# Another opening for a Fourier-mixing and mixture kernel: unfolded stage A, moves within SBUF, four real products, GpSimd for the weights

## The chip, the cores and the metric

The kernel runs on one core of a Trainium2 chip. The metric is device microseconds for one execution. TensorE (PE in the profile, with its weight loads as PEld), VectorE (DVE), ScalarE (ACT) and GpSimd (POOL) each follow an instruction stream of their own. All transfers are issued from SyncE's queue (SP), in order, and run on the core's 16 DMA engines.

## The reference, cut to what matters

Eight sequences of 3008 tokens with 256 features go through a real Fourier transform along the sequence, a complex 256x256 matrix with bias, a soft threshold and the inverse transform. Each token then goes through a two-layer network with a squared ReLU.

```python
X = np.fft.rfft(x, axis=1)                  # x: (8, 3008, 256)
Yr = Xr @ w_r - Xi @ w_i + b_r
Yi = Xr @ w_i + Xi @ w_r + b_i
Yr = np.sign(Yr) * np.maximum(np.abs(Yr) - 0.01, 0)     # Yi likewise
y = np.fft.irfft(Yr + 1j * Yi, n=3008, axis=1)
h = np.maximum(y.reshape(24064, 256) @ w_in, 0)         # w_in: 256 x 2048
out = h * h @ w_out                                     # w_out: 2048 x 256
```

`x`, `w_r`, `w_i` and the biases are float32; `w_in` and `w_out` arrive as float64 and are narrowed on the chip.

## The kernel before, in words

The transform of length 3008 = 47 x 64 is done in stages, each a small matmul with a table. **Stage A** transforms over the 47 indices n1: for a real sequence, 24 frequencies r are enough. **Stage B** transforms over the 64 indices n2; a *pair* is two of the 24 frequencies, so there are 12 pairs (`NPAIR`) for a batch. Then comes the **mix**, the complex matrix as three real products (`MIX`, with the matrices w_r, -w_r-w_i, w_i-w_r in `wmf`, and the sum of the components from `sum_x`), the bias and the threshold (`add_e` and what follows it), a turn of real and imaginary halves into partitions (`zh`), **stage C** (the inverse over n2, table `tM`) and **stage D** (`inverse` or `plan_d`, the inverse over n1). Between A and B (`scr1`, tensors `s<-eva`, `bin<-s`) and between C and D (`scr2`, `s<-evc`, `din<-s`) the data go through DRAM, since rows become partitions.

Before stage A, real sequences are *folded*: the host places rows n1 and 47-n1 side by side (`xp`: 13 groups of up to 24 x 5 = 120 partitions), and `fold` makes their sum and difference on VectorE (L214, L215), so that each part is one matmul with 120 rows.

The network runs in **rounds**. The 104 groups of 5 n2-values form 52 chunks of 470 columns; each chunk takes 8 rounds (`NU`), so there are 416 and two more for the lag. In a round, `mm1` multiplies the chunk (`xt`) with two blocks of `w_in` into `ph` (L186 to L188, three products of high and low float32r parts), `squares` and `sums` prepare seven products (`g`), their high part `gh` (L793) and low part `gl` (L801) follow in the next round, and `mm2` (`po`) multiplies them with seven sums of `w_out` blocks (`wo`) two rounds after the first. Stages A, B, C, D of the batches 2 to 7 (B to D of batch 1) are placed into these rounds by a plan written out by hand: `at(r, place, do)` puts a step in round r at one of the places load, a1, p1, v1, p2, a2, v2, and the loop at the end runs them in that order. p1 lies behind `mm1`, p2 behind `mm2`, a1 behind `gh`, a2 behind the round's squares, v2 last on VectorE. The loop is under `tc.manual_schedule()`: each engine gets its instructions in program order.

`start()` is the **opening**: everything that must be there before round 0. It loads tables and weights, does stages A to C of batch 0, stage A of batch 1, the inverse of the first chunk, and turns `w_in` and `w_out` into high and low parts. It is written as generators that are interleaved (`stages_b` in the middle, `weights` every second step, `stage_a(1)` from the last pair on and behind it), but it stands outside of `manual_schedule`, so the scheduler of the framework settles each engine's order. Its matmuls are plain float32 (L409, L223, L440, L456). A weight piece (512 KB of float64) takes one DMA, one `Abs` on ScalarE (L318), four integer operations on VectorE (L319 to L324), and then either a split in two (`w_in`, L180 and L181) or two copies, four differences and a split (`w_out`, L362 to L367, L180, L181), with ScalarE for casts and VectorE for the rest. There are eight pieces of each.

A DMA tile named `t`, `ev` or `w` in the text is a rotating buffer: a new use waits until the last use of that buffer is over. In PSUM the opening has eight banks (`pst`), the rounds have two for the stages (`ps_f`).

Of the kernel before, what the change touches and what calls it, by code (L numbers as in the profile page):

```python
# [34 lines left out]
P = 128  # L35
S = 3008
# [43 lines left out]

def _cs(num, den):

    num = np.asarray(num) % den
    ang = 2.0 * np.pi * num / den
    c, s = np.cos(ang), np.sin(ang)
    c = np.where((4 * num) % (2 * den) == den, 0.0, c)
    s = np.where((2 * num) % den == 0, 0.0, s)
    return c, s


def tables():
# [39 lines left out]
    return dict(t_a=ta.astype(np.float32), t_b=tb.astype(np.float32), t_m=tm.astype(np.float32),  # L131
# [15 lines left out]
def fft_mix_moe(ctx: ExitStack, tc: tile.TileContext, xp, w_r, w_i, b_r, b_i,  # L147
                w_in, w_out, t_a, t_b, t_m, t_d, sgn, outT):
    nc = tc.nc
    B = xp.shape[0]  # L150
# [24 lines left out]
    wi_ = [ctile(f"wi{k}", [P, 2, DFF], F32R) for k in range(2)]  # L175
    wo_ = []

    def split(src, hi, lo):

        nc.scalar.copy(hi, src)  # L180
        nc.vector.tensor_sub(lo, src, hi.bitcast(F32))  # L181
# [16 lines left out]
    def load_x(b, i, t):  # L198
        nc.sync.dma_start(out=t, in_=xp[b].rearrange("g p d -> p g d")[:t.shape[0], i, :])
# [76 lines left out]
    def start():  # L276

        with ExitStack() as own:
            sb = own.enter_context(tc.tile_pool(name="sb0", bufs=2))
            pp = own.enter_context(tc.tile_pool(name="ps0", bufs=8, space=bass.MemoryType.PSUM))  # L280

            def tl(tag, shape=(P, 512), dt=F32, bufs=2, name=None):
                return sb.tile(list(shape), dt, tag=tag, name=name or tag, bufs=bufs)
# [3 lines left out]

            tA = tl("tA", (120, 4, 120), bufs=1)
            tM = tl("tM", (P, P), bufs=1)
            wmf = [tl(f"wmf{k}", (P, 3, D), bufs=1) for k in range(2)]  # L290

            def load_mix():
                nc.sync.dma_start(out=tB[:, :5], in_=t_b[:, :5])
                yield
                wr = tl("ld", bufs=4, name="wr").rearrange("p (k e) -> p k e", k=2)
                wi = tl("ld", bufs=4, name="wi").rearrange("p (k e) -> p k e", k=2)
# [4 lines left out]
                nc.sync.dma_start(out=sg, in_=sgn)  # L301
                nc.sync.dma_start(out=tM, in_=t_m)
                yield
                for k in range(2):
                    nc.scalar.copy(wmf[k][:, 0], wr[:, k])
                    nc.vector.scalar_tensor_tensor(wmf[k][:, 1], wr[:, k], -1.0, wi[:, k],
                                                   op0=ALU.mult, op1=ALU.subtract)
                    nc.vector.tensor_sub(wmf[k][:, 2], wi[:, k], wr[:, k])
                nc.sync.dma_start(out=tB[:, 5:], in_=t_b[:, 5:])
                nc.sync.dma_start(out=tD, in_=t_d)  # L310
                yield

            def narrow(t, h):
# [4 lines left out]
                nc.scalar.activation(h, hi.bitcast(F32), AF.Abs)  # L318
                nc.vector.tensor_scalar(h, h, F_MIN, F_MAX, op0=ALU.max, op1=ALU.min)  # L319
# [7 lines left out]
            def load_w(src, use):  # L327

                h = tl("w32")
                if src.dtype == F32:  # L330
                    nc.sync.dma_start(
                        out=h.rearrange("p (f n) -> p f n", f=2) if len(src.shape) == 3 else h, in_=src)
                    yield
                else:
                    t = tl("w64", (P, 512, 2), U32)
# [6 lines left out]
                    narrow(t, h)  # L342
                use(h)

            def load_win():
                for c in range(DFF // 512):
                    for k in range(2):
                        s = slice(512 * c, 512 * c + 512)

                        def use(h, k=k, s=s):  # L350
                            split(h, wi_[0][:, k, s], wi_[1][:, k, s])

                        yield load_w(w_in[k * P:(k + 1) * P, s], use)

            def load_wout():
                wo_.extend(ctile(f"wo{k}", [P, NU, NPR, P], F32R) for k in range(2))
                wv = w_out.rearrange("(f p) e -> p f e", p=P)
                for j in range(NU):
                    def use(h, j=j):
                        a = h.rearrange("p (f e m) -> p f e m", f=2, e=2)  # L360
                        w7 = tl("w7", (P, NPR, P), bufs=1)
                        nc.scalar.copy(w7[:, 0:3:2], a[:, :, 0])  # L362
                        nc.scalar.copy(w7[:, 1], a[:, 1, 1])
                        nc.vector.tensor_add(w7[:, 4], a[:, 0, 1], a[:, 1, 1])
                        nc.vector.tensor_sub(w7[:, 6], w7[:, 4], a[:, 0, 0])
                        nc.vector.tensor_sub(w7[:, 5], a[:, 0, 0], a[:, 0, 1])
                        nc.vector.tensor_sub(w7[:, 3], a[:, 1, 0], w7[:, 6])  # L367
                        split(w7, wo_[0][:, j], wo_[1][:, j])

                    yield load_w(wv[:, 2 * j:2 * j + 2, :], use)  # L370

            def rolling(pieces):

                last = None
                for p in pieces:
                    next(p)
                    if last is not None:
                        for _ in last:
                            pass
                        yield  # L380
                    last = p
                for _ in last:
                    pass
                yield

            def stage_a(b):
                scratch1(b)
                if b == 0:
                    st = [const.tile([P, 8, 512], F32, tag=f"wo{k}", name=f"x0{k}") for k in range(2)]
                    xv = xp[b].rearrange("g p d -> p g d")  # L390
                    for g0, g1 in ((0, 1), (1, 2), (2, 4), (4, 6), (6, 8), (8, 10), (10, 12), (12, 13)):
                        n = NR * GROUPS[g0][1]
                        k = g0 // 8
                        nc.sync.dma_start(out=st[k][:n, g0 - 8 * k:g1 - 8 * k, :], in_=xv[:n, g0:g1, :])
                    yield
                for i, (g, w) in enumerate(GROUPS):
                    n = NR * w
                    tab = 0 if w == W else 2
                    if b == 0:
                        t = st[i // 8][:n, i % 8, :]  # L400
                    else:
                        t = tl("ld", bufs=4, name="xin")[:n]
                        load_x(b, i, t)
                    f = tl("f")[:n]
                    fold(f, t)
                    o = pst("psa")[:n]
                    for c in range(2):
                        cs = slice(c * D, c * D + D)
                        nc.tensor.matmul(o[:, cs], tA[:n, tab + c, :n], f[:, cs], start=True, stop=True)  # L409
                    e = tl("ev", bufs=4, name="eva")[:n]  # L410
                    nc.scalar.copy(e, o)
                    store_a(b, i, e)
                    yield

            def stages_b():
                scratch2(0)
                xs, zs, got = {}, {}, {}

                def load(i):
                    got[i] = tl("ld", bufs=4, name="bin")  # L420
                    load_b(0, i, got[i])

                load(0)
                load(1)
                for i in range(NPAIR + 2):
                    if i + 2 < NPAIR:
                        load(i + 2)
                    if i < NPAIR:
                        ps = pst("psb")
                        points_b(ps, i, got.pop(i))  # L430
                        x = xs[i] = tl("x", (P, 3, 2, P))
                        take_b(x, ps)
                        sum_x(x)
                        yield i
                    if 0 <= i - 1 < NPAIR:
                        x = xs.pop(i - 1)
                        p = pst("psm1"), pst("psm2")
                        for comp, mat, bank, half in MIX:
                            for k in range(2):
                                nc.tensor.matmul(p[bank][:, half * D:half * D + D], x[:, comp, k],  # L440
# [414 lines left out]
```

## Time and profile before

| | |
|---|---|
| three runs, median (lowest, highest) | 2757.08 us (2751.55, 2760.26) |
| profiled execution | 2757.75 us, of which the span is 2756.0 |
| granted TensorE clock, mean | 0.982 |
| busy PE, DVE, ACT, POOL | 2621.9, 2160.0, 2050.9, 0.2 us |
| DMA | 163.94 MB, 59 GB/s over the span |
| first matmul of round 0 | at 164.41 us |

The page gives each engine's busy time and share, then the span in 40 slices, the DMA queues, the chain of work that ended last, and the costliest groups of instructions. A group reads: line, engine, operation, output<-inputs, shapes, count | busy us, mean ns of one | idle time of the engine before them and what ended it. A row of the timeline reads: start, duration, engine, line, operation, tensors, count, and in brackets the idle time before it with what ended it. A row of windows reads: stretch, its length, busy us (count) of PE, PEld, DVE, ACT and POOL, mean granted clock, share of time in which the 16 DMA engines were busy, GB/s.

### The profile page before, as it was taken

The numbers are of one execution on the slowest core, as the hardware profiler recorded it, in microseconds if no ns is written. First come the engines' busy times: TensorE is split into PE (matmuls) and PEld (weight loads), VectorE is DVE, ScalarE is ACT, GpSimd is POOL, SyncE is SP. The second block draws the span as 40 slices with busy tenths as digits, with TensorE's granted clock in tenths as the row PEclk, the third lists the DMA queues.
The fourth block names the chain that finished last, engine by engine and source line by source line (L and its number), as shares of the span: only waits on it lengthen the run. The fifth ranks groups of instructions, "written<-read, shape, count | busy, mean of one in ns | idle before, by whom it ended". The sixth has DMA issues, their size and how long they took to land.

```text
span 2756.0 us, 45108 instructions
## 1 busy us (share of the span) xinstructions
PE 2621.9 (95%) x17832; PEld 2443.3 (89%) x17832; DVE 2160.0 (78%) x3383; ACT 2050.9 (74%) x2917; POOL 0.2 (0%) x4
## 2 busy tenths in 40 slices
PE   5679999999999999999999999999999999999998
PEld 4469999999889999999999999899989999999998
DVE  5858888788877888878887888778888888777776
ACT  4757778678777778777777777777777777766665
POOL 0000000000000000000000000000000000000000
PEclk8789999999999999999999999999999999999999
DMA  7431113111121112311122111311113111000000
GB/s 218 141 103 34 52 45 96 53 49 44 57 90 41 54 44 68 93 37 53 41 89 70 38 46 48 95 52 51 46 59 100 42 36 55 26 28 24 19 26 18
DMA packets 128245, 163.94 MB, mean 59 GB/s; under 512 B 10931, under 2 KB 87971, under 8 KB 128035
## 3 DMA queue, kind: packets, MB, share of 16 engines
q1 hardware_dynamic: 128035, 161.06, 19.5%
q8 instruction: 142, 2.33, 0.4%
q14 instruction: 68, 0.56, 0.1%
HBM read 86.04 MB, written 74.97 MB: 58 GB/s over the span
## 4 chain that ended last, share of the span: by engine, by line
PE 65%; DVE 15%; ACT 14%; issue 3%; DMA 3%; SPq 0%; ACTq 0%; DVEq 0%
PE ph L186 9%; PE ph L187 9%; PE ph L188 8%; PE po L188 8%; PE po L187 8%; PE po L186 8%; ACT gh L793 6%; DVE gl L801 3%; PE psd L261 2%; PE psb L223 2%; ACT g L743 2%; DVE g L750 2%; ACT g L744 2%; PE psm L188 2%; PE psm L186 2%
## 5 line engine op out<-in xcount | busy, mean ns | idle before, releaser
L801 DVE TENSOR_TENSOR gl<-g,gh 128x1652 fp32r<-128x1652 f32 (+1 forms) x416 | 770.4, 1852 | 384.1 <-ACT gh L793 384.1
L793 ACT CAST gh<-g 128x1652 fp32r<-128x1652 f32 (+1 forms) x416 | 645.7, 1552 | 438.7 <-DVE g L752 241.8
L186 PE MATMUL po<-gh,wo 128*128 128x236 f32 (+1 forms) x2912 | 811.6, 279 | 2.2 <-DVE o L775 1.4
L187 PE MATMUL po<-gl,wo 128*128 128x236 f32 (+1 forms) x2912 | 803.8, 276 | 2.4 <-DVE gl L801 2.4
L188 PE MATMUL po<-gh,wo 128*128 128x236 f32 (+1 forms) x2912 | 805.0, 276 | 0.0
L186 PE MATMUL ph<-xt,wi 128*128 128x470 f32 (+1 forms) x1664 | 634.0, 381 | 6.1 <-ACT g L743 5.3
L187 PE MATMUL ph<-xt,wi 128*128 128x470 f32 (+1 forms) x1664 | 623.7, 375 | 3.8 <-DVE xt L697 3.8
L188 PE MATMUL ph<-xt,wi 128*128 128x470 f32 (+1 forms) x1664 | 619.0, 372 | 0.0
L186 PEld LDWEIGHTS po<-gh,wo 128*128 128x128 f32 x2912 | 559.9, 192 | 10.3 <-DVE o L775 2.7
L187 PEld LDWEIGHTS po<-gl,wo 128*128 128x128 f32 x2912 | 559.5, 192 | 7.7 <-DVE gl L801 2.8
L188 PEld LDWEIGHTS po<-gh,wo 128*128 128x128 f32 x2912 | 561.3, 193 | 0.0
L743 ACT ACTIVATE g<-ph 128x472 f32<-128x472 f32 (+1 forms) x832 | 417.4, 554 | 105.0 <-PE ph L188 100.3
L744 ACT ACTIVATE g<-g 128x944 f32<-128x944 f32 (+1 forms) x416 | 408.8, 983 | 13.2
L186 PEld LDWEIGHTS ph<-xt,wi 128*128 128x128 f32 x1664 | 316.1, 190 | 40.0 <-ACT g L743 8.6
L188 PEld LDWEIGHTS ph<-xt,wi 128*128 128x128 f32 x1664 | 314.5, 189 | 39.0
L187 PEld LDWEIGHTS ph<-xt,wi 128*128 128x128 f32 x1664 | 317.0, 190 | 33.0 <-DVE xt L697 6.1
L750 DVE TENSOR_TENSOR g<-g 128x472 f32<-128x472 f32 (+1 forms) x416 | 266.7, 641 | 41.5 <-ACT g L744 28.0
L752 DVE TENSOR_TENSOR g<-g 128x236 f32<-128x236 f32 (+1 forms) x416 | 166.5, 400 | 14.4
L751 DVE TENSOR_TENSOR g<-g 128x236 f32<-128x236 f32 (+1 forms) x416 | 166.5, 400 | 14.3
L188 PE MATMUL psm<-wm,xl 128*128 128x256 f32 x504 | 142.2, 282 | 15.4 <-DVE xl L606 15.4
L186 PE MATMUL psm<-wm,xh 128*128 128x256 f32 x504 | 140.0, 278 | 0.0
L187 PE MATMUL psm<-wm,xh 128*128 128x256 f32 x504 | 139.9, 277 | 0.0
(97 smaller groups left out, 2797.4 us busy)
## 6 DMA issues: line engine op xcount, KB each, us to landing
bin<-s SPq DMA_DIRECT2D x96, 256.0 KB
s<-evc SPq DMA_DIRECT2D x96, 256.0 KB
s<-eva SPq DMA_DIRECT2D x96, 240.0 KB
din<-s SPq DMA_DIRECT2D x96, 240.0 KB
xin<-in_xp_dram SPq DMA_DIRECT2D x84, 240.0 KB
outT_dram<-o SPq DMA_DIRECT2D x96, 118.0 KB
outT_dram<-o SPq DMA_DIRECT2D x96, 117.0 KB
w<-in_moe_w_in_dram SPq DMA_DIRECT2D x8, 512.0 KB
```

What stands on the lines that cost most here:

```text
L186: nc.tensor.matmul(out, l0, r0, start=start, stop=False, **kw)
L187: nc.tensor.matmul(out, l0, r1, start=False, stop=False, **kw)
L188: nc.tensor.matmul(out, l1, r0, start=False, stop=stop, **kw)
L223: nc.tensor.matmul(ps[:, k, :, q, :], tv[:, q, k], tB[:, 0:r + 2:r + 1], start=True, stop=True)
L261: nc.tensor.matmul(ps[:, k, part], t[:n, s:s + P], tD[:n, tab + part, :n], start=True, stop=True)
L743: nc.scalar.activation(g[:, t:4:2, :m], ph[:, :, t * t0:t * t0 + m], AF.Relu)
L744: nc.scalar.activation(g[:, 0:4, :m], g[:, 0:4, :m], AF.Square)
L750: nc.vector.tensor_sub(g[:, 4:6, :m], g[:, 1:4:2, :m], g[:, 0:2, :m])
L751: nc.vector.tensor_sub(g[:, 6, :m], g[:, 3, :m], g[:, 4, :m])
L752: nc.vector.tensor_sub(g[:, 1, :m], g[:, 6, :m], g[:, 2, :m])
L793: nc.scalar.copy(gg[k][0][:, :, :m], hid[k][:, :, :m])
L801: nc.vector.tensor_sub(gg[k][1][:, :, :m], hid.pop(k)[:, :, :m], gg[k][0][:, :, :m].bitcast(F32))
```

## The change

**Opening.** All of `start()` now stands under `manual_schedule`, so the order is the program's. Stage A of batches 0 and 1 is *unfolded*: the host places their tokens as `xu`, 94 partitions (47 n1 times two neighbouring n2) by 32, and one matmul with a new table `tU` (94 x 96) makes all four parts of two columns, 16 of them a batch. For batch 0 the results go by DMA from the copy `ev` straight into `xb` in SBUF, two moves of 96 rows into 4 partitions each, in place of `scr1`; for batch 1 they go into `scr1`, also two a block. The three products of the mix become four, as one accumulation over 512 columns in float32r parts (`w3`, holding -w_i, w_r, w_i), with the bias added by two matmuls of one row (`one`, `rows`). `sum_x`, `add_e` and `wmf` leave the opening; the three matrices of the later batches are made at its end (`tables_main`). Differences and low parts of weights and tables move from VectorE to GpSimd. A weight piece now advances by one step in each pass of the loop (`weights`), and one new piece is begun in each. Stage A of batch 1 runs one block in each pass from the third on, with its x loads two in each of the first eight. The copies out of PSUM alternate between ScalarE and VectorE (`copy`). `ev` has three buffers instead of four. `wo_` becomes 16 tiles, whose places hold the x tiles of batch 1 before.

**Rounds.** In `plan_a` the matmuls move from p1 to p2 of the same round, and the eviction from a2 of that round to a1 of the next one (the last group stays at a2).

```diff
+def plain_rows():
+    n2 = np.arange(N2).reshape(-1, 2)
+    return ((64 * np.arange(N1)[:, None, None] + 47 * n2.T[None]) % S).reshape(2 * N1, N2 // 2)
...
             pp = own.enter_context(tc.tile_pool(name="ps0", bufs=8, space=bass.MemoryType.PSUM))
+            own.enter_context(tc.manual_schedule())
...
+            x0 = [const.tile([P, nq, D], F32, tag=f"wi{k}", name=f"x0{k}") for k in range(2)]
+            def load_x0(k, parts):
+                for g0, g1 in parts:
+                    nc.sync.dma_start(out=x0[k][:2 * N1, g0:g1, :], in_=xu[0, :, nq * k + g0:nq * k + g1, :])
+            def load_x1():
+                i = len(x1)
+                if i < nq:
+                    x1.append(const.tile([P, 2, D], F32, tag=f"wo{i % 2}{i // 2}", name=f"x1{i}"))
+                    nc.sync.dma_start(out=x1[i][:2 * N1], in_=xu[1, :, 2 * i:2 * i + 2, :])
+            def loads():
+                dma = nc.sync.dma_start
+                dma(out=tU, in_=t_u)
+                load_x0(0, ((0, 2), (2, 4), (4, 8), (8, 12), (12, 16)))
+                for k in range(2):
+                    dma(out=raw[k][:, 1], in_=w_r[k * P:k * P + P, :])
+                    dma(out=raw[k][:, 2], in_=w_i[k * P:k * P + P, :])
+                load_x0(1, ((0, 8), (8, 16)))
...
             def narrow(t, h):
                 nc.scalar.activation(h, hi.bitcast(F32), AF.Abs)
+                yield
                 nc.vector.tensor_scalar(h, h, F_MIN, F_MAX, op0=ALU.max, op1=ALU.min)
...
+                    nc.scalar.copy(wi_[0][:, k, s], h)
+                    yield
+                    nc.gpsimd.tensor_sub(wi_[1][:, k, s], h, wi_[0][:, k, s].bitcast(F32))
...
+                    w7 = tl("w7", (P, NPR, P), bufs=2)
+                    nc.scalar.copy(w7[:, 0:3:2], a[:, :, 0])
+                    nc.scalar.copy(w7[:, 1], a[:, 1, 1])
+                    nc.gpsimd.tensor_add(w7[:, 4], a[:, 0, 1], a[:, 1, 1])
+                    nc.gpsimd.tensor_sub(w7[:, 5], a[:, 0, 0], a[:, 0, 1])
+                    nc.gpsimd.tensor_sub(w7[:, 6], w7[:, 4], a[:, 0, 0])
+                    nc.gpsimd.tensor_sub(w7[:, 3], a[:, 1, 0], w7[:, 6])
+                    yield
+                    nc.scalar.copy(wo_[0][j], w7)
+                    yield
+                    nc.gpsimd.tensor_sub(wo_[1][j], w7, wo_[0][j].bitcast(F32))
...
             def stage_a(b):
+                if b:
+                    scratch1(b)
+                    v = scr1[b].rearrange("r n (c d) -> (n c) r d", c=2)
+                for i in range(nq):
+                    t = x1[i][:2 * N1] if b else x0[i // 8][:2 * N1, 2 * (i % 8):2 * (i % 8) + 2, :]
+                    o = pst("psa")[:4 * NR]
+                    nc.tensor.matmul(o, tU, t.rearrange("p k d -> p (k d)"), start=True, stop=True)
+                    e = tl("ev", bufs=3, name="eva")[:4 * NR]
+                    copy(i, e, o)
+                    for k in range(2):
+                        q = 8 * i + 4 * k
+                        nc.sync.dma_start(out=v[q:q + 4] if b else xb[q:q + 4], in_=e[:, k * D:k * D + D])
+                    yield
...
+            def pair_mix(i):
+                h, l = xs.pop(i)
+                p = pm[i] = pst("psm")
+                for n in range(2):
+                    nc.tensor.matmul(p, one, rows[n], start=n == 0, stop=False)
+                for c in range(2):
+                    for k in range(2):
+                        w = slice(D - D * c, 3 * D - D * c)
+                        mm3(p, (h[:, k, c], l[:, k, c]), (w3[0][:, k, w], w3[1][:, k, w]),
+                            False, c + k == 2)
...
+            loads()
+            a0, a1 = stage_a(0), stage_a(1)
+            for i, _ in enumerate(a0):
+                if i == 3:
+                    nc.sync.dma_start(out=tB[:, :5], in_=t_b[:, :5])
+                if i == 9:
+                    tables_start()
+                if i == 12:
+                    weights()
+            more_loads()
+            weights()
...
+            for n in range(NPAIR + 3):
+                if 0 <= n - 2 < NPAIR:
+                    pair_z(n - 2)
+                if n < NPAIR:
+                    pair_b(n)
+                if 0 <= n - 1 < NPAIR:
+                    pair_mix(n - 1)
+                if n >= 3:
+                    pair_c(n - 3)
+                    pair_out(n - 3)
+                load_x1()
+                load_x1()
+                if n >= 2:
+                    next(a1)
+                if 0 <= n - 2 < NPAIR:
+                    pair_turn(n - 2)
+                if n == NPAIR - 2:
+                    nc.sync.dma_start(out=tD, in_=t_d)
+                    next(late)
+                if n == NPAIR + 1:
+                    next(late, None)
+                weights()
+            inv = inverse(0, xt)
+            next(inv)
+            next(a1, None)
+            weights()
+            for _ in inv:
+                next(a1, None)
+                weights()
+            for _ in a1:
+                weights()
+            while weights():
                 pass
...
-                at(r + 1, "p1", points)
-                at(r + 1, "a2", out)
+                at(r + 1, "p2", points)
+                at(*((r + 2, "a1") if i + 1 < len(GROUPS) else (r + 1, "a2")), out)
```

`pair_z` is the threshold of a pair (one operation on ScalarE, one on VectorE), `pair_b` its stage B with the split, `pair_turn` the turn (half of it now on VectorE), `pair_c` and `pair_out` its stage C and the store. A *pass* below is one step n of that loop.

More of the change, by code (lines that the diff above doesn't have):

```diff
@@ L286, in pst @@
                 return pp.tile([P, 512], F32, tag="f", name=name)
[L288 to L296, printed above, removed]
+            tM = tl("tM", (P, P))
@@ new lines, in start @@
+            tU = tl("tU", (2 * N1, 4 * NR))
+            row = tl("t", name="row")[:1]
+            rows = [tl(f"row{k}", (1, 2 * D), F32R) for k in range(2)]
+            ones = tl("z", name="ones")[:1, :P]
+            one = tMs[:1, 0, :]
+            xb = tl("xb", (P, NR, D))
+            nq = N2 // 4
+            x0 = [const.tile([P, nq, D], F32, tag=f"wi{k}", name=f"x0{k}") for k in range(2)]
+            x1 = []
+            def load_x0(k, parts):
+                for g0, g1 in parts:
+                    nc.sync.dma_start(out=x0[k][:2 * N1, g0:g1, :], in_=xu[0, :, nq * k + g0:nq * k + g1, :])
@@ new lines, in loads @@
+            def loads():
[6 more added lines that the diff above has]
+                load_x0(1, ((0, 8), (8, 16)))
+                dma(out=row[:, :D], in_=b_r[None, :])
+                dma(out=row[:, D:], in_=b_i[None, :])
+                nc.vector.memset(ones, 1.0)
+                nc.scalar.copy(one, ones)
@@ L341, in load_w @@
                     yield
[L342 to L346, printed above, removed]
-                    for k in range(2):
[L348 to L370, printed above, removed]
@@ L372, in rolling @@
-            def rolling(pieces):
-                last = None
-                for p in pieces:
-                    next(p)
[L377 to L384, printed above, removed]
-            def stage_a(b):
[L387 to L394, printed above, removed]
-                    yield
[L396 to L413, printed above, removed]
@@ new lines, in start, with weights @@
+            pending = itertools.chain((win(c, k) for c in range(DFF // 512) for k in range(2)),
+                                      (wout(j) for j in range(NU)))
+            going = []
+            def weights(begin=True):
+                for p in list(going):
+                    if next(p, going) is going:
+                        going.remove(p)
+                p = next(pending, None) if begin else None
+                if p is not None:
+                    next(p)
+                    going.append(p)
+                return bool(going)
@@ L463, in inverse, with pair_out @@
+            def pair_out(i):
+                ev = tl("ev", bufs=3, name="evc")
+                copy(i, ev, pc.pop(i))
+                store_c(0, i, ev)
             def inverse(c, xt):
                 for u in range(len(chunks[c])):
-                    t = tl("ld", bufs=4, name="din")
+                    t = tl("xl", bufs=2, name="din")
                     load_d(c, u, t)
```

201 lines of the change are left out of this document (101 added, 100 removed).

## The prediction

> **What bounds the kernel now.** I read the page first for the whole, then the table of windows for the opening, then its chain and timeline, then the waits of the main loop.
>
> ```profile
> span 2756.0 us, 45108 instructions
> 0.00:10.00 10.00, 4.52 (x12) 3.20 (x13) 3.54 (x10) 3.04 (x4) 0.20 (x4) 1.00 0.79 195
> 10.00:20.00 10.00, 8.90 (x39) 6.21 (x38) 6.52 (x19) 1.75 (x3) 0.00 (x0) 1.00 0.95 244
> 90.00:100.00 10.00, 4.61 (x22) 3.48 (x22) 9.47 (x20) 7.24 (x14) 0.00 (x0) 0.86 0.62 201
> 130.00:140.00 10.00, 3.78 (x6) 1.79 (x6) 0.00 (x0) 1.85 (x4) 0.00 (x0) 0.50 0.51 144
> 164.40:2756.00 2591.60, 2519.22 (x17448) 2367.94 (x17448) 2056.75 (x3156) 1961.21 (x2748) 0.00 (x0) 0.99 0.17 52
> ```
>
> Each row of windows has the stretch, its length, the busy us of PE, PEld, DVE, ACT and POOL, then the granted clock, the DMA share and GB/s. From 164.4 us on PE is busy 2519 of 2592 us: the main loop is PE's, and nothing there gains more than some 70 us. The opening has three limits in turn: transfers (0 to 37; share 0.95 at 10), VectorE (9.47 of 10 us at 90), and then a tail in which everyone waits for stage A of batch 1 and for the inverse stage (PE 3.78 of 10 us at half clock at 130).
>
> ```profile
> 1.25 4.68 SPq L394 DMA_DIRECT2D x<-in_xp_dram  x8
> 19.25 0.42 DVE L214 TENSOR_TENSOR f<-x 96x256 f32<-96x256 f32 x1 [0.27 <-PE psa L409]
> 37.51 3.75 PE L223 MATMUL psb<-tB,bin 128*128 128x128 f32 x16 [16.50 <-DMA bin<-s]
> 130.15 2.08 PE L456 MATMUL psc<-zh,tM 128*128 128x512 f32 x2 [1.10 <-ACT zh L452]
> 164.41 0.48 PE L186 MATMUL ph<-xt,wi 128*128 128x470 f32 x1 [0.72 <-ACT eva L411]
> ```
>
> These rows of the timeline (start, duration) mark the joints: the last x rows of batch 0 are folded at 19, stage B starts at 37.5, the last pair leaves PE at 132.2, and the main loop begins at 164.4. The sum is made against the profiled execution, 2757.75 us with 1.75 around its span; the median shown is 2757.08, so the two are one number. 0.3%, about 8 us, is what a measurement here can tell from no change.
>
> **The change, part by part.** What decides is how many of the 16 DMA engines a transfer gets. Three answers on stretches in which one transfer ran alone:
>
> ```profile
> DMA packets 135, 0.25 MB, mean 34 GB/s; under 512 B 15, under 2 KB 15, under 8 KB 135
> q1 hardware_dynamic: 135, 0.25, 12.5%
> xin<-in_xp_dram SPq DMA_DIRECT2D x1, 240.0 KB
> ...
> q1 hardware_dynamic: 132, 0.25, 11.2%
> din<-s SPq DMA_DIRECT2D x1, 240.0 KB
> ...
> q1 hardware_dynamic: 272, 0.26, 10.5%
> s<-evc SPq DMA_DIRECT2D x1, 256.0 KB
> ```
>
> Beyond its rows (120, 120 and 256) each leaves a few tiny packets: 15, 12 and 16. I read them as one closing packet for each engine used. A transfer with 120 rows on both sides then ran on 15 engines, one that joins 24 outer rows to 120 ran on 12, one with 128 on 16. In all three every engine has the same number of rows, and the count is the largest up to 16 that allows it on both sides.
>
> The new x loads have 94 rows (two of 47). 94 splits evenly over 2 only. The moves into xb write 4 partitions from 96 rows, so 4. If an uneven split were possible (six rows each), the loads would have 16; no row shows one, so I take 2, at three chances in four.
>
> [...]
>
> One engine's rate:
>
> ```profile
> 38.00:39.00 1.00, 1.00 (x7) 1.00 (x6) 0.00 (x0) 0.00 (x0) 0.00 (x0) 0.50 0.98 379
> ```
>
> 379 GB/s over 16 engines busy 0.98 is 24.2 GB/s for each. The lone x load above gives 0.25 MB in 12.5% of 16 x 7.2 us, 17.4 GB/s. The new loads are a standing queue of long rows, nearer to the first: 24.2 taken.
>
> *Loads of batch 0.* One engine has 47 rows of 32 KB, 1.540 MB, with 33 KB of mix weights and 18 KB of tU: 1.591 MB / 24.2 = 66 us. SP issues all of them before any move, as it does now (1.25, x8). SP's own issue time (0.37 to 0.78 us, rows below; some 134 in the opening, under 70 us in all) stays under the transfers'. With a start at 2.5 the loads end at 68 us, where now the last fold comes at 19. The unfolded stage drops 26 folds of 0.42 us from VectorE, which was waiting for loads: nothing on the path.
>
> *Moves.* 16 blocks, two moves each of 96 KB. They queue behind the loads on the shared engines, and only three `ev` buffers are there, so from the fourth block on copies and SP's stores stand still until 68. The price of one move has no row. From below: 24,576 B on each of four engines, 1.0 us. From above: the 4 partitions take no more than one engine's stream to 8 partitions does now, 98,304 B / 24.2 = 4.1 us. Up to six moves go to different partitions, though in order on the same engines, so neither end is nearer: 2.6. 32 x 2.6 = 83, with 2 to land: stage B starts at 153 instead of 37.5 (103 to 200 by the ends). What goes is the store, the load back and its wait, all inside that 37.5.
>
> [...]
>
> *Loop of stage B, first half.* Two x tiles of batch 1 are loaded in each of the first eight passes, on the same two engines. Each pass also loads a weight piece through two buffers; its `Abs` stands in ACT's fixed order, so what is queued behind it (the next pass's threshold, copies and turns) waits when the piece is late. One engine then carries, until the last x tile: 16 x 96,256 B = 63.6 us, eight weight shares of 32,768 B = 10.8, twelve moves out for stage A of batch 1 = 12.2, five stores of stage C = 3.4, tables 1.9. Sum 92: at 245. If PE's clock falls to half between passes, as at 130 now, a pass of 6.4 (below) becomes 12.8 against 11.5: at most 10 us more, inside the ends of the moves.
>
> *Loop, second half.* The three engines in one pass:
>
> ```profile
> 49.89 1.05 PE L223 MATMUL psb<-tB,bin 128*128 128x128 f32 x8
> 48.92 1.13 PE L456 MATMUL psc<-zh,tM 128*128 128x512 f32 x2 [0.85 <-ACT zh L452]
> 169.53 0.38 PE L187 MATMUL ph<-xt,wi 128*128 128x470 f32 x1
> 169.74 0.38 PE L188 MATMUL ph<-xt,wi 128*128 128x470 f32 x1
> L322 DVE SCALAR_TENSOR_TENSOR w<-w,w 128x512 uint32<-128x512 uint32 x16 | 10.9, 684 | 0.0
> L319 DVE TENSOR_SCALAR w<-w 128x512 f32<-128x512 f32 x16 | 6.8, 422 | 4.2 <-ACT w L318 4.2
> L366 DVE TENSOR_TENSOR w<-w 128x128 f32<-128x128 f32 x8 | 2.3, 285 | 0.0
> L181 DVE TENSOR_TENSOR wo<-w,wo 128x896 fp32r<-128x896 f32 x8 | 8.7, 1085 | 0.1
> L444 ACT ACTIVATE t<-e,neg 128x512 f32<-128x512 f32 x12 | 8.7, 721 | 1.9 <-DVE e L238 1.9
> L452 ACT ACTIVATE zh<-z,sg 64x256 f32<-64x256 f32 x24 | 12.1, 505 | 0.3
> L318 ACT ACTIVATE w<-w 128x512 f32<-128x512 f32 x16 | 10.8, 674 | 6.0 <-DMA w<-in_moe_w_in_dram 4.1 <-DMA w<-in_moe_w_out_dram 1.6
> L180 ACT CAST wo<-w 128x896 fp32r<-128x896 f32 x8 | 7.5, 937 | 2.2 <-DVE w L367 2.1
> L362 ACT COPY w<-w 128x256 f32<-128x256 f32 x8 | 3.2, 402 | 1.3 <-DVE w L324 1.1
> ```
>
> PE: 1.05 for B, 14 matmuls of 512 columns in the mix (0.21 x 512/470 = 0.23 each, 3.2; the bias rides on two of them), 1.1 for C and as much for stage A: 6.4 us. VectorE keeps z, the low part and a copy (as L322, 0.68 each), two half copies (under 0.42 each) and the narrowing (2 x 0.68, 2 x 0.42): 5.1. The bias adds, the component sum and the weights' differences leave it. ACT: the threshold, a cast and an eviction (at most 0.72 each), two turns (1.0), the piece (`Abs` 0.67, cast 0.94, two copies up to 0.4): 5.6 at most. PE covers both. GpSimd has no arithmetic row: its five operations for an output piece took VectorE 2.2 us (1.085 and four of 0.285), so it may be up to three times slower before it fills a pass of 6.4, and its results are needed only rounds after the loop: nothing, from either end. Passes 9 to 14 are three full ones, then 5.3, 5 and 2: with the last `Abs` 32 us, at 277.
>
> *Tail.* Thirteen of the sixteen blocks of stage A of batch 1 are now inside the loop, so behind the last pair come only copy 0.6, store, load, inverse:
>
> ```profile
> 132.87 0.37 SPq L211 DMA_DIRECT2D s<-evc  x1
> 135.56 0.78 SPq L251 DMA_DIRECT2D din<-s  x1
> 147.70 0.78 SPq L251 DMA_DIRECT2D din<-s  x1
> 152.30 1.12 PE L261 MATMUL psd<-tD,din 120*128 120x120 f32 x8 [0.31 <-DMA din<-s]
> ```
>
> 2.7 from store to load, 4.6 to the matmul, 1.1, and four short operations and a split on ACT and VectorE, 0.4 to 0.65 each, partly side by side, with the second half behind: 3. That is 12 in all. The main loop begins at 289 instead of 164.4: **+125**, in which the tail gives back 20 (32 to 12).
>
> *Stage A in the main loop.* Its matmuls move behind the second product, its eviction into the next round:
>
> ```profile
> PE psa L187 <- DVE fl L557: 17.2, 13, 2.6
> PE psa L186 <- ACT fh L553: 1.3, 2, 0.9
> PE psc L186 <- DVE dx L269: 10.9, 8, 1.5
> ```
>
> The first two waits (total, times, longest) can go, 18.5 us; VectorE's lateness stays, and the third row shows what meets it next: the two PSUM banks, which psa now holds across the round's end. Between 0 and 18.5 I take **-10**. In the rounds with stage C too, psa needs a bank that ACT empties only in the same round: 12 such rounds, under 1 us each, is why not more.
>
> Sum: 2757.75 + 125 - 10 = **2873**.
>
> **The rivals.** *Moves cheap.* At 1.0 us a move, stage B starts at 103: 2823. For it: a single engine's rate above. Against: four partitions. *Moves dear.* At 4.1: 2920.
>
> *Loads spread over 16 engines, moves on four at 1.0 us* (faster). The x loads end near 18 as now, 13 blocks of 2.04 follow, stage B starts at 47; nine full passes of 6.4 and six short ones (the first three 11, the last three 12) put the last pair at 128 and the main loop at 140: -24, and -10, 2724. For it: the loads now run at share 0.95 and more; against it: even shares in every row. Break-even with before is stage B at about 81 us, so the load of batch 0 ending near 52. With moves at 2.6 the same loads give 2779, slower.
>
> *The main loop gains nothing:* +10 on any of these.
>
> **How the numbers follow.** Two-engine loads hold 0.75: moves near 2.6 0.35 (2845 to 2900), cheap 0.15, dear 0.25. Spread loads: cheap moves 0.20, dear 0.05. Predicted 2873. Range 2722 to 2920: it reaches to the faster rival and leaves out the slowest moves and a lower rate of an engine. Spread loads with cheap moves give faster 0.17 and, where half of the moves' lower price is missed, same 0.03; slower 0.80 is the rest.
>
> **What would show it.** Right: between 8 and 68 us a DMA share near 0.13 at about 50 GB/s, PE almost idle, ACT and VectorE waiting for the moves; two closing packets for each of the 23 x loads; first `psb` between 100 and 200; passes of about 11 us until the x tiles are in, then 6 to 7; VectorE no longer above 9 of 10; less than 15 us between the last `psc` and the inverse's matmul; the psa wait gone. Wrong: a share above 0.7 in the first 20 us and `psb` before 60 us, which makes it faster.

## The result and the profile after

The changed kernel takes **2856.16 us** (median of four runs, 2853.96 to 2857.14) against 2754.76 us before on the same chip (2751.55 to 2760.26): ratio **1.0365, 95% interval [1.0345, 1.0385]**. The profiled execution took 2853.96 us, 2851.7 of it the span. The forecast was 2873.

The same view as before, the table of stretches (length, busy PE, PEld, DVE, ACT, POOL, granted clock, DMA share, GB/s), of the changed kernel:

```profile
30.00:40.00 10.00, 4.79 (x6) 0.96 (x4) 0.00 (x0) 0.00 (x0) 0.00 (x0) 1.00 0.13 52
90.00:100.00 10.00, 0.00 (x0) 0.00 (x0) 3.01 (x4) 1.61 (x3) 0.00 (x0) 1.00 0.27 74
270.16:2851.70 2581.54, 2519.20 (x17448) 2364.01 (x17448) 2057.75 (x3156) 1959.16 (x2748) 1.21 (x1) 1.00 0.17 52
```

At 30 us the DMA share is 0.13 of 16 engines, that is 2.1 engines, at 52 GB/s, where before it was 0.95 and 244 GB/s at 10. At 90 us, when almost only moves run, it is 0.27, 4.3 engines. No engine is busy for half of its time in either stretch. In the main loop PE is busy for the same 2519 us as before, in 10 us less.

The joints, from the timeline of the changed kernel (start, duration, engine, line, operation, in brackets the idle time before and what ended it):

```profile
14.00 8.33 SPq L336 DMA_DIRECT2D raw<-in_w_i_dram  x1
32.19 8.85 SPq L338 DMA_DIRECT2D row<-in_b_r_dram  x1
42.39 21.39 SPq L473 DMA_DIRECT2D xb<-eva  x4
117.50 3.75 PE L237 MATMUL psb<-tB,xb 128*128 128x128 f32 x16 [30.52 <-DMA xb<-eva]
238.78 2.04 PE L517 MATMUL psc<-zh,tM 128*128 128x512 f32 x2 [1.37 <-DVE zh L512]
270.16 0.73 PE L200 MATMUL ph<-xt,wi 128*128 128x470 f32 x1 [3.82 <-DVE eva L458]
```

and the waits of the opening and of PE in the main loop (total, times, longest):

```profile
DVE eva L458 <- DMA xb<-eva: 82.8, 6, 55.3
ACT eva L458 <- DMA xb<-eva: 69.0, 5, 49.8
...
PE psm L202 <- DVE xl L684: 15.9, 13, 2.2
PE psc L200 <- DVE dx L283: 11.3, 9, 1.4
PE ph L200 <- ACT g L821: 10.7, 12, 2.4
PE psa L200 <- ACT evc L726: 2.9, 1, 2.9
```

Stage B starts at 117.5 instead of 37.5, the last stage C matmul ends at 240.8 instead of 132.2, the main loop begins at 270.2 instead of 164.4. The wait of psa for `fl` (17.2 us before) is gone. The wait of `ph` for ScalarE's `g`, 10.7 us now, was half as long before:

```profile
PE ph L186 <- ACT g L743: 5.3, 5, 2.3
```

The opening costs 105.8 us more, the main loop 10.1 less; the spans of the two profiled executions differ by 95.7, the medians by 101.4.

### The profile page after: what moved, and what is told of

The parts are those of the page before. It is cut to its first block, busy times and chain, and to the rows that moved or that the text cites. A ratio compares the mean times of both kernels' runs of the same rounds, so it can differ in the third digit from the quotient of the medians.

```text
span 2851.7 us, 45021 instructions
## 1 busy us (share of the span) xinstructions
PE 2654.9 (93%) x17816; PEld 2438.2 (85%) x17816; DVE 2152.3 (75%) x3301; ACT 2032.6 (71%) x2885; POOL 52.8 (2%) x60
## 3 DMA queue, kind: packets, MB, share of 16 engines
q1 hardware_dynamic: 127282, 158.34, 18.5%
## 4 chain that ended last, share of the span: by engine, by line
PE 55%; DVE 17%; ACT 15%; DMA 6%; issue 4%; SPq 2%; POOL 0%; ACTq 0%; DVEq 0%; POOLq 0%
PE ph L200 7%; PE ph L201 7%; PE ph L202 7%; PE po L202 7%; PE po L201 7%; PE po L200 7%; ACT gh L871 7%; DVE gl L879 4%; DVE g L828 3%; ACT g L822 3%; ACT g L821 3%; DMA xb<-eva 2%; PE psm L202 2%; PE psb L237 2%; PE psd L275 2%
## 5 line engine op out<-in xcount | busy, mean ns | idle before, releaser
L200 PE MATMUL ph<-xt,wi 128*128 128x470 f32 (+1 forms) x1664 | 635.9, 382 | 14.7 <-ACT g L821 10.7
L200 PE MATMUL psm<-wm,xh 128*128 128x256 f32 (+1 forms) x552 | 165.9, 300 | 22.7 <-ACT xh L484 22.7
L202 PE MATMUL psm<-wm,xl 128*128 128x256 f32 (+1 forms) x552 | 165.9, 300 | 16.1 <-DVE xl L684 15.9
L201 PE MATMUL psm<-wm,xh 128*128 128x256 f32 (+1 forms) x552 | 164.0, 297 | 0.0
```

The costliest lines, as they stand in the source:

```text
L200: nc.tensor.matmul(out, l0, r0, start=start, stop=False, **kw)
L201: nc.tensor.matmul(out, l0, r1, start=False, stop=False, **kw)
L202: nc.tensor.matmul(out, l1, r0, start=False, stop=stop, **kw)
```

## The experiments

Four theories stood against one another: the x loads run on few engines because of their 94 rows; the moves are the cost; the end of the opening is held by GpSimd or by the order of the queues; the main loop's gain is the shift's own. The kernel before ran beside the versions on the same chip each time, with medians of 2753.28 to 2756.06 us. The tail is counted in this section from the start of the last stage C matmul to the first `ph`, 31.4 us in the changed kernel and 34.3 before (the expectations and the forecast count it from that matmul's end, 2 us less).

**Rows of the loads.** `xu` gets 96 partitions on the host, the last two zero, and the loads take 96 (or 95) of them; the matmul still reads 94. Batch 0 alone, batch 1 alone, both, both with 95:

```diff
-    xu = x[:2, plain_rows()]
+    xu = np.zeros((2, 96, N2 // 2, D), x.dtype)
+    xu[:, :2 * N1] = x[:2, plain_rows()]
-    out=x0[k][:2 * N1, g0:g1, :], in_=xu[0, :, ...]      # batch 0
+    out=x0[k][:96, g0:g1, :], in_=xu[0, :96, ...]
-    out=x1[i][:2 * N1], in_=xu[1, :, ...]                # batch 1
+    out=x1[i][:96], in_=xu[1, :96, ...]
```

> One edit to the changed kernel: the x loads of batch 0 carry 96 rows (two rows of zeros) instead of 94. Theory (94 rows run on two DMA engines): the loads of batch 0 then run on 16, end near 20 us instead of 68, and stage B starts near 70 instead of 117.5; the rest is as in the changed kernel: 2856 - 45 = about 2811 us. Rival (the moves into four partitions set the start of stage B): it starts later than 100, and the time stays within 10 us of 2856.

> One edit to the changed kernel: only the x loads of batch 1 carry 96 rows. Theory: the passes with x loads fall from 11.9 us to the 6.4 us of TensorE, seven or eight of them: 2856 - 40 = about 2816 us, with stage B still starting near 117. Rival (a pass is slow because every engine now follows a written order): passes stay above 10 us and the time stays near 2856.

> Both x loads carry 96 rows. Theory: the two gains add, as they lie one behind the other: 2856 - 85 = about 2770 us, which is 15 us over the kernel before, because 17 us in the tail (GpSimd) stay. Rival (the written order or the moves within SBUF are what costs): 2830 us or more. The x loads then leave 16 closing packets each instead of 2.

> Both x loads carry 95 rows, one row of zeros. If rows are split evenly (95 = 5 x 19), the loads run on five engines, at 2.5 times the rate of the changed kernel, about 130 GB/s: batch 0 is in near 30 us, and a tile of batch 1 costs an engine 1.6 us instead of 4: 2856 - 70 = about 2785 us, between 94 and 96 rows. If six rows went to each engine whatever is left over, 94, 95 and 96 rows would all be alike.

| rows of batch 0, 1 | median us | ratio to before | stage B starts | between stage B's first and last C |
|---|---|---|---|---|
| 94, 94 | 2856.16 | 1.0365 [1.0345, 1.0385] | 117.5 | 121.3 |
| 96, 94 | 2809.43 | 1.0207 [1.0190, 1.0224] | 70.3 | 122.1 |
| 94, 96 | 2817.45 | 1.0235 [1.0219, 1.0250] | 115.9 | 86.0 |
| 95, 95 | 2789.26 | 1.0130 [1.0115, 1.0146] | 84.9 | 90.7 |
| 96, 96 | 2772.46 | 1.0071 [1.0056, 1.0087] | 72.4 | 85.9 |

Stretches with loads, with 95 rows in both batches first, then with 96 in both:

```profile
10.00:20.00 10.00, 9.70 (x12) 3.19 (x12) 0.00 (x0) 0.58 (x1) 0.00 (x0) 1.00 0.33 130
```

```profile
12.00:17.00 5.00, 5.00 (x7) 1.70 (x6) 0.00 (x0) 0.00 (x0) 0.00 (x0) 1.00 1.02 229
```

A share of 0.13, 0.33 and 1.02 is 2.1, 5.3 and 16 engines. Two rows of zeros more, and the loads leave two engines; one row gives five. Of the 101 us lost, 84 (2856.16 - 2772.46; 81 by the two ratios) are these two rows. Each batch pays at its own place: batch 0 ahead of stage B, batch 1 in the passes of the loop. In the changed kernel three passes take 18.8 us (127.00 to 145.82 below), the next six 71.9, that is 12.0 each (145.82 to 217.74):

```profile
127.00 1.05 PE L237 MATMUL psb<-tB,xb 128*128 128x128 f32 x8
...
145.82 1.05 PE L237 MATMUL psb<-tB,xb 128*128 128x128 f32 x8
...
182.61 1.05 PE L237 MATMUL psb<-tB,xb 128*128 128x128 f32 x8
...
217.74 1.05 PE L237 MATMUL psb<-tB,xb 128*128 128x128 f32 x8
```

A pass takes 6.25, from the third on, in the version with batch 1 alone:

```profile
137.27 1.05 PE L237 MATMUL psb<-tB,xb 128*128 128x128 f32 x8
143.53 1.05 PE L237 MATMUL psb<-tB,xb 128*128 128x128 f32 x8
```

2, 5 and 16 are the largest numbers up to 16 that divide 94, 95 and 96. The measured 2.1, 5.3 and 16 engines agree with the even split that the prediction read from 120, 24 and 128 rows.

All that follows is built on the version with 96 rows for both, 2772 us, where the first `ph` stands 25 us later than before (189.6): stage B starts 35 later, the way to the last C is 7 shorter (85.9 for 92.6), the tail 3 (31.4 for 34.3).

**Moves: buffers, partitions, way.** Three edits:

```diff
 # six buffers in batch 0
-e = tl("ev", bufs=3, name="eva")
+e = tl("w32", ...) if b == 0 and i % 2 else tl("ev", ...)
 # destination partitions 32 apart
-out=xb[q:q + 4]
+out=xb[q // 4:q // 4 + 97:32]
 # through DRAM, then four loads of 128 partitions
-out=v[q:q + 4] if b else xb[q:q + 4]
+out=v[q:q + 4]
+for q in range(0, NR, 6):
+    nc.sync.dma_start(out=xb[:, q:q + 6], in_=v[:, q:q + 6])
```

> Edit to the 96-row version of both batches (2772 us, stage B at 72 us, the 32 moves of batch 0 spread over some 50 us): odd blocks of batch 0 take their copy from three buffers that are idle until the weights start, so six buffers instead of three stand before the moves. If the wait for a free copy (VectorE 39 us, ScalarE 40 us) is a matter of few buffers, the moves run at the rate of four engines, 96 KB in 1.0 us by 24.2 GB/s an engine: 32 us for the 32, stage B at about 50 and the kernel at about 2750. If the moves themselves are the limit (67 to 70 GB/s in the slices from 20 to 50 us, 1.4 us each), more buffers only let the copies run ahead: stage B at 70 to 73, kernel 2770 to 2774.

> Edit to the 96-row version: the four partitions that a move writes lie 32 apart (m, m+32, m+64, m+96) instead of side by side. The rows of xb stand in another order, so batch 0 is not the transform; the work is the same. If four neighbouring partitions share a way into SBUF that holds the moves at 67 to 70 GB/s, the moves get quicker: 32 us for the 32 by four engines at 24.2 GB/s, stage B at about 50, kernel about 2750. If the four engines or the buffers are the limit, nothing changes: stage B at 70 to 74, kernel 2770 to 2775.

> Edit to the 96-row version: batch 0 goes from stage A to stage B through DRAM (32 stores of 96 KB, then four loads of 128 partitions), as batch 1 does, not by moves within SBUF. If the moves on four engines are what holds stage B until 72 us, it now starts where TensorE allows: 16 blocks of 2.02 us from 5 us on end at 38, a store and a load behind that make 44 to 48; kernel 2772 - 26 = about 2746. If a write of four rows' worth costs the same wherever it goes, stage B stays at 65 to 75 and the kernel at 2765 to 2775.

The stretches in which moves (or stores) run almost alone; with 96 rows, with six buffers, with partitions 32 apart, and through DRAM:

```profile
30.00:40.00 10.00, 6.10 (x7) 1.18 (x6) 1.37 (x2) 0.58 (x1) 0.00 (x0) 1.00 0.26 67
```

```profile
30.00:40.00 10.00, 1.85 (x3) 0.22 (x1) 3.70 (x5) 3.98 (x7) 0.00 (x0) 1.00 0.26 79
```

```profile
30.00:40.00 10.00, 4.42 (x5) 1.17 (x6) 1.37 (x2) 0.58 (x1) 0.00 (x0) 1.00 0.27 57
```

```profile
25.00:35.00 10.00, 7.59 (x9) 1.79 (x7) 2.41 (x4) 3.62 (x7) 0.00 (x0) 1.00 0.28 96
```

In all four a little over four engines are busy (shares of 0.26 to 0.28, 4.2 to 4.5), and the rate of each differs: 67, 79, 57 and 96 GB/s make 96 KB last 1.47, 1.24, 1.72 and 1.02 us. The kernels took 2766.47 us (ratio 1.0038 [1.0026, 1.0051], stage B at 65.6), 2782.38 (1.0099 [1.0082, 1.0116], 86.3) and 2761.15 (1.0021 [1.0012, 1.0031], 58.4). None fits its theory whole. The buffers gave 6 us, not the 20 of "a matter of few buffers". Partitions lying apart (batch 0 is then not the transform, the work is the same) made the moves slower, against both theories. The way through DRAM gave 11 us of 26: its stores are quicker than the moves (1.02 us against 1.47), but still run on four engines (4.5) and hold the copies until 47 us, though PE was done with stage A at 33.

**The tail.** First the inverse of the first chunk ahead of what is left of weights, matrices and stage A; then all GpSimd work back on VectorE:

```diff
-            inv = inverse(0, xt)          # interleaved with a1, weights()
-            ...
+            for _ in inverse(0, xt): pass
+            for _ in a1: weights()
+            while weights(): pass
+            next(late, None)
```

```diff
-nc.gpsimd.tensor_sub(...)   # tables_main and weights, with split(..., nc.gpsimd)
+nc.vector.tensor_sub(...)
```

> Edit to the 96-row version: behind the loop, the inverse of the first chunk stands ahead of the rest of stage A, of the weights and of the three matrices of the later batches (in the version it is interleaved with them). The tail between the last stage C matmul and the first ph was 29.3 us. If it is the waits for GpSimd and the work interleaved in ScalarE's and VectorE's order that make the tail, it falls to 13 to 18 us; what stands behind then meets round 0, where it can give back a part: kernel 2756 to 2766. If the tail is the chain of C, its store, load and D itself, it stays at 27 or more and the kernel at 2770 or above.

> Edit to the 96-row version: all differences and low parts of weights and tables on VectorE, as before the change; GpSimd does nothing. If GpSimd lengthens the tail (it is waited for by ScalarE, and a VectorE operation of two SBUF inputs takes 2.3 to 2.5 us beside it instead of 0.65), the tail falls from 29 to 12 to 18 us, while the passes of the second half grow from 6.26 to about 7 us, as VectorE gets 7.3 us of work in each: first ph at 185 to 190, kernel 2766 to 2773. If GpSimd's help is needed (VectorE becomes the bound of passes and tail), passes of 8 us or more and the kernel at 2785 or above.

The tail of the changed kernel in its timeline (what lies between is left out):

```profile
242.90 0.68 DVE L458 COPY evc<-psc 128x512 f32<-128x512 f32 x1
243.60 0.38 SPq L225 DMA_DIRECT2D s<-evc  x1
250.61 0.40 ACT L427 COPY w<-w 128x256 f32<-128x256 f32 x1 [3.98 <-POOL wo L438]
251.68 0.57 ACT L458 COPY eva<-psa 96x512 f32<-96x512 f32 x1
252.27 1.27 SPq L473 DMA_DIRECT2D s<-eva  x2
253.72 0.84 SPq L265 DMA_DIRECT2D din<-s  x1
257.54 2.03 PE L275 MATMUL psd<-tD,din 120*128 120x120 f32 x8 [14.19 <-DMA din<-s]
262.79 2.42 DVE L195 TENSOR_TENSOR xt<-dx,xt 128x470 fp32r<-128x470 f32 x1 [0.65 <-ACT xt L194]
```

The store of the last pair is issued at 243.6, the load that needs it only at 253.7: ahead of it in SP's queue stands a store of stage A, whose copy stands in ScalarE's queue behind a weight copy that waits 4 us for GpSimd. So one wait passes through three queues.

Without GpSimd the same stretch reads:

```profile
167.22 0.68 DVE L458 COPY evc<-psc 128x512 f32<-128x512 f32 x1
167.93 0.37 SPq L225 DMA_DIRECT2D s<-evc  x1
171.86 0.83 SPq L265 DMA_DIRECT2D din<-s  x1
175.57 2.04 PE L275 MATMUL psd<-tD,din 120*128 120x120 f32 x8 [14.19 <-DMA din<-s]
```

The load now follows its store by 3.9 us instead of 10.1, but the last copy itself, behind the three matrices on VectorE, comes 8 us after its matmul (156.82 and 2.04). The wait for `din` is 14.19 us in both; the tail is 28.2 instead of 31.4 and the kernel 2770.13 us (1.0050 [1.0035, 1.0065], which overlaps the interval of the version with 96 rows). GpSimd lengthened the tail by some 3 us and saved VectorE nothing that the passes needed: they stay at 6.25. My theory of GpSimd as the cause of the tail fell.

With the inverse first the tail is 24.4, between the two expectations, and the kernel stays at 2775.42 (1.0069 [1.0054, 1.0084]). Behind the last stage C matmul, which ends at 158.1 there, stand:

```profile
159.98 0.68 DVE L458 COPY evc<-psc 128x512 f32<-128x512 f32 x1
174.60 0.65 DVE L195 TENSOR_TENSOR xt<-dx,xt 128x470 fp32r<-128x470 f32 x1 [0.65 <-ACT xt L194]
180.50 0.73 PE L200 MATMUL ph<-xt,wi 128*128 128x470 f32 x1 [4.49 <-ACT w L428]
```

The first chunk is ready 17.1 us behind that matmul. The first `ph` comes 5.2 us later still: its wait ends with a copy of a weight piece on ScalarE. So the chain itself takes 17 us, 2 of them before its first copy, and the leftover holds `ph` even from behind it. The first 19 us of the main loop with the inverse first, and of the version with 96 rows:

```profile
180.50:200.00 19.50, 8.07 (x20) 6.61 (x21) 1.46 (x3) 7.16 (x13) 13.15 (x13) 0.59 0.18 54
```

```profile
189.64:209.00 19.36, 15.81 (x72) 13.54 (x72) 8.24 (x12) 9.32 (x12) 1.20 (x1) 0.80 0.22 62
```

PE works 8 instead of 16 us there, while GpSimd, busy 13 us, finishes the weights and the matrices. Its longest wait is one for ScalarE's first operation on `ph`, which stands behind the casts of the matrices in ScalarE's order:

```profile
PE ph L200 <- ACT g L815: 11.4, 1, 11.4
```

What the leftover costs ahead of the main loop it costs in it when it is moved there.

**The main loop's part alone**, in the kernel before:

```diff
-                at(r + 1, "p1", points)
-                at(r + 1, "a2", out)
+                at(r + 1, "p2", points)
+                at(*((r + 2, "a1") if i + 1 < len(GROUPS) else (r + 1, "a2")), out)
```

> The kernel before with nothing but the change in the main loop: stage A's matmuls behind mm2 and its eviction in the next round. The main loop of the changed kernel took 2581.5 us against 2591.6. If that is the shift's work, it comes alone too: 10 us, kernel about 2745. If it came from the other opening (what is left over at its end, other buffers), the kernel stays at 2752 to 2757.

2743.92 us, ratio **0.9956 [0.9944, 0.9969]**: faster than both kernels. Its main loop:

```profile
161.89:2742.60 2580.71, 2517.41 (x17448) 2362.93 (x17448) 2057.38 (x3156) 1960.18 (x2748) 0.00 (x0) 1.00 0.17 52
```

2580.7 against 2591.6 before and 2581.5 in the changed kernel: the gain belongs to the shift, whatever opening stands ahead of it.

**Two versions of all together.** The first takes the way through DRAM, starts the weights two passes earlier and stage A of batch 1 with the loop; the second also writes with 24 outer rows (columns of tU in another order), has no GpSimd work, loads x of batch 1 during stage A, and puts the leftover behind the inverse:

```diff
+                if 8 <= i < 12: load_x1()                # second version
+                if 12 <= i < 15: weights()
-                if i == 12: weights()
-                if n >= 2: next(a1)
+                if n >= 1: next(a1, None)                # first: every n, and one block ahead of the loop
-    tu = tu.reshape(2 * N1, 4 * NR)                      # second version
+    tu = tu.transpose(0, 1, 4, 2, 3).reshape(2 * N1, 4 * NR)
+    v = scr1[b][:, q:q + 2, :].rearrange("r n (c d) -> r (n c) d", c=2)
```

> The version through DRAM, and the end of the opening relieved: the weight pieces start two passes earlier and stage A of batch 1 runs in the passes from the first on, so that three steps of weights and no block of stage A are left behind the loop. If the tail of 29 us is that leftover work in the queues of ScalarE, VectorE and SP ahead of the inverse, it falls to 14 to 18 us and the kernel to about 2732 to 2736. If the tail is the chain of stage C, its store, the load and D, it stays at 25 to 29 and the kernel at the time of the version through DRAM.

> The 96-row version with both batches through DRAM, and the columns of tU in another order (frequency first, then the four parts), so that a store of 96 KB has 24 outer rows instead of 4. The loads used 2, 5 and 16 engines for 94, 95 and 96 rows, transfers of 24 outer rows 12, of 4 outer rows 4: each time the largest divisor up to 16. If that is the rule, these stores use 12 engines, 96 KB in 0.4 us at 20 GB/s an engine, stage B starts a store and a load behind the last block of stage A (33 us), at 42 to 46 instead of 58. If four rows of destination were only slow for being many small stores, it stays at 55 or more. Also in it: no work on GpSimd, weight pieces started two passes earlier, x of batch 1 loaded during stage A, and the leftover of weights behind the inverse of the first chunk. With passes of 6.26 us as before, the last stage C is 86 us behind the start of stage B; if the tail of 29 us was leftover work in the queues ahead of the inverse, it falls to 15 to 20: first ph at 143 to 152, the kernel at 2727 to 2736. If the tail is the chain of stage C, store, load and D, it stays at 25 or more: 2738 to 2745.

The first took 2770.18 us (1.0053 [1.0039, 1.0066]), slower than its parent at 2761, by an error of mine that the timeline shows:

```profile
73.79 1.99 PE L467 MATMUL psa<-x,tU 94*96 94x512 f32 x2 [40.95 <-DMA x<-in_xu_dram]
75.57 1.91 PE L237 MATMUL psb<-tB,xb 128*128 128x128 f32 x8
```

The block of stage A placed ahead of the loop waits for x of batch 1, and stage B, in order behind it, starts at 75.6 instead of 58.4. Its tail is 24.0 instead of its parent's 31.4, between the two expectations.

The second took 2755.30 us, ratio 0.9998 [0.9989, 1.0007]: no better than before and 11 us behind the shift alone. Its stage B starts at 56.7, not at 42 to 46:

```profile
43.35 0.66 ACT L381 ACTIVATE w<-w 128x512 f32<-128x512 f32 x1 [8.65 <-DMA w<-in_moe_w_in_dram]
43.91 0.57 ACT L458 COPY eva<-psa 96x512 f32<-96x512 f32 x1
...
56.68 3.75 PE L237 MATMUL psb<-tB,xb 128*128 128x128 f32 x16 [24.58 <-DMA xb<-s]
```

The weights that I started earlier stand ahead of the last copies of stage A on ScalarE and wait there 8.7 us for their own transfer. Whether the wider stores alone would bring stage B to 45 us stays open. The tail is 24.8 and the first `ph` at 170.5, still behind the 161.9 to 164.4 of the old opening: both expectations, 2727 to 2736 and 2738 to 2745, were missed.

## Why the prediction was right, and where not

| step | forecast us | measured us |
|---|---|---|
| loads of batch 0 end | 68 | 67 |
| from there to stage B | 85 | 51 |
| stage B to the end of stage C | 124 | 123.3 |
| tail, from the end of the last stage C matmul | 12 | 29.3 |
| main loop, against before | -10 | -10.1 |

The end of the loads is read from the sizes of the packets between 66 and 67 us and between 67 and 68: the last loads have packets of 8 KB, the moves of 1 KB, and the last one of 8 KB lies in the first stretch. The third row is from the chain of the changed kernel (start, duration, what): the first copy that waits for a free buffer waits for moves that land at 69.6.

```profile
DMA packets 55, 0.06 MB, mean 61 GB/s; under 512 B 2, under 2 KB 54, under 8 KB 54
DMA packets 64, 0.06 MB, mean 62 GB/s; under 512 B 3, under 2 KB 64, under 8 KB 64
43.23 26.41 DMA xb<-eva
```

- *Loads of batch 0.* Right in mechanism and size: two engines, 52 GB/s, an end at 67. Padding the rows takes it away (16 engines, 229 GB/s). One detail was wrong: SP's issue time was to stay under the transfers'. It was held (8.33 and 8.85 us for single issues, rows above), and the first move was issued only at 42.4. The first moves landed at 69.6, about when forecast all the same, behind the loads. That moves and loads share engines stood in no row of the kernel before; this landing, 26.4 us after the issue, is what the run shows of it.
- *Moves.* The mechanism was right (four engines, 4.3 by the share at 90 us, the copies standing still behind three buffers), the term was mis-sized: 2.6 us each, the middle of 1.0 and 4.1, made 83 for 32. Thirteen blocks, 26 moves, took the 48 us from the first free buffer (69.7) on, 1.8 each, and with little beside them they go at 1.24 to 1.47 into neighbouring partitions. Whether more buffers would help beside the narrow loads was not run. The lower end (an engine's rate) was the nearer one: moves into neighbouring groups of partitions ran at 67 to 79 GB/s together, far above the limit that I let in from above (24.2), and with partitions lying apart they did worse (57).
- *Loop, first and second half.* 123.3 for 124 together, and the limit of the slow passes was the forecast one: the 96 rows of batch 1 alone turn 12.0 into 6.25, where PE is busy all the time. But the split was wrong. Not the first eight passes were slow: stage B of the ninth starts at 182.6, 65 us behind the first and not 92, and the sixth to the eleventh pass took the 12.0. That the sum fits to 0.7 us is in part luck.
- *GpSimd, "nothing, from either end".* Not right, but small: 3 us at the tail, where its results were needed before the main loop after all, through ScalarE's order.
- *Tail.* The step that failed. It added up one chain, copy, store, load, inverse, and left out what the program places among it: matrices, five weight pieces and three blocks of stage A, in fixed order on ScalarE, VectorE and SP. Of the 17 us too few, by the version with the inverse first (its tail without that edit is the same 31.4), 7 were work ahead of the inverse, 5 were work ahead of the first `ph`, and 5 were the chain itself, which takes 17.1 and not 12. The sign "less than 15 us between the last `psc` and the inverse's matmul" failed with it: 16.7. The rule that every queue passed must be counted was applied to the loads and not here.
- *Main loop.* Right, and shown alone by the shift in the kernel before. The size was a choice between 0 and 18.5, so the fit to 0.1 us is luck, and what ate the rest was not the named one: the wait of `psc` for `dx` is 11.3 (10.9 before), while that of `ph` for `g` grew from 5.3 to 10.7.

Two errors stood against each other: moves 34 too dear, tail 17 too cheap; with 1 at the loads, 0.7 at the loop and 0.1 at the main loop the sum comes to the 2854 of the profiled execution. That 2873 lies as near as 17 us is luck; the side and the range held because the largest term, the two-engine loads (84 us of 101 by the padded rows), was right in both batches. The rival "loads spread over 16 engines" was wrong about 94 rows, but its engines are those of 96 rows. With its dearer moves it gives 2779, measured 2772; that nearness is luck too, as by such moves stage B would start near 103 (18 + 83 + 2), not at 72.4, and the tail in it was 12, not 29.

## What to carry to other kernels

Look at the number of DMA engines that every new transfer gets before anything else: 94 rows got 2.1 here, 95 rows 5.3 and 96 rows 16, and two rows of padding were worth 84 us, more than all other parts of the change. Where engines run in program order, a tail is not its chain (17.1 us here) but all that stands ahead of each link in each queue (29.3 us with it); work that is moved off the chain but is still waited for in the same queue (weights to GpSimd, the leftover behind the inverse, weights started early) came back here as a wait a few us later (4.0, 11.4 and 8.7 us). Try the parts of a large change one by one: the small edit in the main loop alone was the only faster kernel.

## What the runs showed of the hardware that I had not expected

- Some VectorE operations between SBUF tiles took up to 3.7 times as long beside a GpSimd operation: the narrowing's `SCALAR_TENSOR_TENSOR` of 128x512 has a median of 0.69 us and a maximum of 2.49 in the changed kernel, against 0.68 to 0.69 in all 16 before, its shift (a `TENSOR_SCALAR`, L384) a maximum of 1.41 against 0.43 before, and the split of 128x470 took 2.42 us (row above) against 0.65 in the version without GpSimd. In the version with 96 rows a `SCALAR_TENSOR_TENSOR` of 2.44 us, from 172.43 on, ends 0.55 us behind a GpSimd subtraction (172.07, 2.25 us). The threshold's operation of the same kind, which reads PSUM, stayed at 0.68 to 0.69 in the changed kernel, also in the three of its twelve that ran beside GpSimd (at 215.74, 222.26 and 231.74).
- SP's issues themselves got slow while the loads ran on two engines: 8.3 us for one (`raw<-in_w_i_dram`, 14.00) that takes 0.45 when the loads run on 16. SP's next command starts at 22.37, behind it.
- Moves from SBUF to SBUF ran at 13 to 19 GB/s an engine (share and rate of the rows above), stores to DRAM, at a share of 0.28, at 21 (96 GB/s), loads from DRAM at 24.6 (95 rows in both batches: 130 GB/s at a share of 0.33). With all 16 engines busy the same loads ran at 14 an engine (229 GB/s at a share of 1.02), so eight times the engines gave 4.4 times the rate of 94 rows (52 GB/s). Destination partitions 32 apart were slower (1.72 us) than neighbours (1.47); why is open.
